# Half 0 alone ahead of the first gate: a reordered start of a block-attention and gated-expert kernel

## The chip, the cores and the metric

The kernel runs on one core of a Trainium2 chip. The metric is the device time of one execution in microseconds (us). Durations of single instructions come from one profiled execution, in which each engine's instructions are recorded: PE (TensorE) multiplies matrices, DVE (VectorE), ACT (ScalarE) and POOL (GpSimd) work elementwise, and SP (SyncE) issues the DMAs.

## The reference

Two parts follow each other. The first is attention with 4 batches, 8 heads, 768 tokens and a head width of 64: a token sees its neighbours at less than 16 places, and 24 summaries, one for each block of 32 tokens (the maximum of the keys, the mean of the values).

```python
k_sum = k.reshape(B, H, nb, block, D).max(axis=3)
v_sum = v.reshape(B, H, nb, block, D).mean(axis=3)
...
scores_all = np.concatenate([scores_l_m, scores_s], axis=-1)
...
a = a / (np.sum(a, axis=-1, keepdims=True) + 1e-09)
return np.matmul(a, v_all).astype(np.float32)
```

The second takes the attention's output as `x`, with 512 features for each token, mixes every token with the one before it, and applies a squared-ReLU pair of products under a sigmoid gate:

```python
xk = mu_k * x + (1.0 - mu_k) * x_prev
xr = mu_r * x + (1.0 - mu_r) * x_prev
k = np.maximum(xk @ w_k, 0.0)
v = k * k @ w_v
r = 1.0 / (1.0 + np.exp(-(xr @ w_r)))
return (r * v).astype(np.float32)
```

`w_k` is 512 x 1024, `w_v` 1024 x 512, `w_r` 512 x 512.

## The kernel before, in words

**Attention.** The heads go in four pairs, two heads of 64 on 128 partitions. For each batch and pair, `load_set` (L310) loads keys into a tile of the pool `kt` (three tiles) and the values of both halves of the tokens into two tiles of `vx`. It adds the block maxima to the keys (L330 to L342) and the block means to the values. For the first batch the means come from PE (L354, with the values of both halves) and a selecting product (L374), through two banks of `mm`, into `vm` and from there by copies (L380) into both value tiles. One `unit` (L394) is a pair and a half of the tokens (384): it loads the queries, makes scores on PE (L415), adds the mask and takes the minimum on DVE (L426), exponentiates on ACT (L430), inverts the sums on DVE (L437), normalises on POOL (L442), transposes on PE (L449), copies on ACT (L453), multiplies by the values on PE (L462) and copies the result out (L473 or L475). A unit needs its pair's keys and both block summaries.

**Gate and experts.** A batch's half (384 tokens, three tiles of 128) is the unit of the second part. `mixes` (L478) makes the mixed input for the gate (`which` 1) or the experts (`which` 0): for each pair a scaling on ACT or POOL (L485, L488), a multiply-add on DVE (L491), a rounded high part on ACT (L494) and the remainder on DVE (L496). The high and low parts stand in `xs`, sixteen buffers, eight for each call; `xa` is the buffer in between. Every product is the sum of three: high by high, high by low, low by high. A gate tile is 12 matmuls into one bank of `mm` (L508 to L510) and a sigmoid into `z` (L514). `experts` (L517) runs eight steps: a first product of 12 matmuls (L529), ReLU, square, split (L534 to L540), and a second of 9 (L550). Three of the four banks of `mm` hold its accumulators, and the fourth serves the first products and any gate tile in between in turn.

**Weights.** The weights arrive as 64-bit words and are turned into a high and a low part by `weight` (L258): a scaling (ACT or POOL), three operations on DVE (L281, L284, L288), a rounding (ACT or POOL) and a subtraction on DVE (L300), for four pieces of `w_r` and eight each of `w_k` and `w_v`. A raw piece waits in one of three `st`.

**Order.** Nothing is ordered by hand. Every operation goes to a planner with a cost (`LENGTH`), and some with a due time; due times are passed backwards to what an operation needs. The planner walks through time, takes on each engine the operation that can start and is due first, and hands out buffers of a pool in the order in which they were asked for. The result is a fixed order for each engine, which the engines follow with semaphores. In the first batch, before the change, the units are due in the order pair 0 half 0, pair 0 half 1, pair 1 half 0 and so on, at `GATES[0] - 2000 - (7 - 2 * p - h) * FIRST`, and all eight are due before the first gate. Half 1's gate tiles stand between the steps of half 0's experts, at the steps in `BETWEEN`.

Of the kernel before, what the change touches and what calls it, by code (L numbers as in the profile page):

```python
# [12 lines left out]
AF = mybir.ActivationFunctionType  # L13
# [4 lines left out]
B, H, S, D = 4, 8, 768, 64  # L18
DM, DF = 512, 1024
BLOCK, WINDOW = 32, 16  # L20
P = 128
NPAIR = H // 2
NS = S // BLOCK
# [3 lines left out]
NK = LK + NS  # L27
KB = QW + NS
KL = NW * KB + 2 * WINDOW
HW = NW // 2  # L30
NSL = HW // 2
HT = S // 2
NTT = HT // P
NCK, NCV = DM // P, DF // P
# [2 lines left out]


LENGTH = dict(
    score=900, transpose=340, vtrans=200, vpool=900, vsel=240, spread=560, spread_p=900, values=1000, gate=2790, gate32=3720, e1=2090, e1_32=2800,  # L40
    e2a=1400, e2b=700, e2=700, e2_32=2800, e2l_32=930,
    kred=860, kred2=470, kmax=190, kcopy=340, vred=860, mask=204, rc=310, evac=475, mixd=535, sub=475, khv=300,
    result=695, wbits=340, wor=612, wsub=612, tiny=60,
# [4 lines left out]
LATENCY = dict(PE=260, DVE=110, ACT=110, POOL=150, SP=0)  # L48
DMA_NS_PER_BYTE = 1 / 340.0
DMA_FIXED = 2000  # L50
GATES = (36000, 46000)
PERIOD = 52000
STEP = 4800
SLACK = 400
COLD = 25000
WR = 0, 6000
EARLY = 15000
FIRST = 4000
UNITS = 6000
BETWEEN = 1, 2, 3  # L60


class Buf:
# [12 lines left out]
class Plan:  # L76
# [4 lines left out]
    def buf(self, pool):  # L81
        n = self.count[pool]
        self.count[pool] = n + 1
        return Buf(pool, n)

    def op(self, eng, cost, due, emit, reads=(), writes=(), size=0, other=None):

        bufs = []
        for x, _ in list(reads) + list(writes):
            if isinstance(x, Buf) and x not in bufs:  # L90
                bufs.append(x)
        ways = {eng: (LENGTH.get(cost, 0), emit)}
        if other:
            ways[other[0]] = (LENGTH[other[1]], other[2])
        o = Op(len(self.ops), ways, due, bufs, size)
        for x in reads:
            o.deps.update(self.writers.get(x, ()))
        for x in writes:
            o.deps.update(self.writers.get(x, ()))
            o.deps.update(self.readers.get(x, ()))  # L100
        for x in reads:
            self.readers.setdefault(x, []).append(o)
        for x in writes:
            self.writers[x] = [o]
            self.readers[x] = []
        o.deps.discard(o)
        for x in bufs:
            x.users.append(o)
        self.ops.append(o)
        o.name = cost  # L110
        return o
# [88 lines left out]
def tile_kernel(ctx: ExitStack, tc: tile.TileContext, q, k, vT, v, mask, ident, pool, sel, mu, w_k, w_v, w_r, out):  # L200
    nc = tc.nc
# [3 lines left out]
    def tiles(name, n, shape, dtype=F32, pool=const):  # L205
        return [pool.tile(shape, dtype, name=f"{name}{i}") for i in range(n)]

    pools = dict(
        kt=tiles("kt", 3, [P, KL]), qt=tiles("qt", 4, [P, HT]), vx=tiles("vx", 12, [P, S + 1]),
        kg=tiles("kg", 2, [P, 49]), ks=tiles("ks", 2, [P, NS]),  # L210
        vs=tiles("vs", 1, [P, NS]), vm=tiles("vm", 4, [P, P]), sp=tiles("sp", 2, [P, P]),
        y=tiles("y", 4, [P, NSL, NK]), mn=tiles("mn", 4, [P, NSL]), sm=tiles("sm", 3, [P, 2 * NSL]),
        rc=tiles("rc", 3, [P, 2 * NSL]), pts=tiles("pts", 3, [NK, NSL, P]),
        z=tiles("z", 6, [P, DM]), xa=tiles("xa", 4, [P, HT]),
        xs=tiles("xs", 16, [P, HT], F32R), r=tiles("r", 2, [P, HT]),
        kh=tiles("kh", 2, [P, HT], F32R), kl=tiles("kl", 2, [P, HT], F32R),
        st=tiles("st", 3, [P, 1024], U32), we=tiles("we", 1, [P, 512], U32), wc=tiles("wc", 2, [P, 512], U32),
# [4 lines left out]
    op, buf = plan.op, plan.buf  # L222
# [10 lines left out]
    wr_h = const.tile([P, NCK, DM], F32R, name="wr_h")  # L233
    wr_l = const.tile([P, NCK, DM], F32R, name="wr_l")
# [10 lines left out]
        out=om_sb, in0=mu_sb, scalar1=-1.0, scalar2=1.0, op0=ALU.mult, op1=ALU.add), reads=MU, writes=OM)  # L245

    def gate_due(b, hf):
        n = 2 * b + hf
        return GATES[n] if n < 2 else GATES[0] + PERIOD * n

    def e1_due(b, hf, j):
        return (GATES[0] + PERIOD * (2 * b + hf)) + 8400 + STEP * j

    def e2_due(b, hf, j):
        return e1_due(b, hf, j + 1) + 2200
# [51 lines left out]
    def windows(vw):  # L307
        return vw.t[0:NK, 0:S].rearrange("p (w d) -> p w d", d=P)

    def load_set(b, p):  # L310

        e = dict(kt=buf("kt"), vw=[buf("vx") for _ in range(2)])
        kt, vw = e["kt"], e["vw"]
        cuts = [0, HW * KB, KL] if (b, p) == (0, 0) else [0, KL]
        for n, (lo, hi) in enumerate(zip(cuts, cuts[1:])):
            op("SP", "load", None, lambda lo=lo, hi=hi: nc.sync.dma_start(out=kt.t[:, lo:hi], in_=k[b, p, :, lo:hi]),
               writes=[(kt, f"k{n}")], size=P * (hi - lo) * 4)
        e["kparts"] = [(kt, f"k{n}") for n in range(len(cuts) - 1)]
        for hf in range(2):
            op("SP", "load", None, lambda hf=hf: nc.sync.dma_start(  # L320
                out=windows(vw[hf]), in_=v[b, p, :, hf * HW:(hf + 1) * HW]),
               writes=[(vw[hf], "a"), (vw[hf], "b")], size=NK * HW * 512)

        def blocks():
# [2 lines left out]
        kg, ks, vm = buf("kg"), buf("ks"), buf("vm")  # L327
        cuts = [0, HW, NW] if len(cuts) > 2 else [0, NW]
        for n, (lo, hi) in enumerate(zip(cuts, cuts[1:])):
            op("DVE", "kred2" if len(cuts) > 2 else "kred", None, lambda lo=lo, hi=hi: nc.vector.tensor_reduce(  # L330
                out=kg.t[:, 4 * lo:4 * hi].rearrange("p (j c) -> p j c", c=4),
                in_=blocks()[:, lo:hi, 0:QW].rearrange("p j (a c) -> p j a c", c=16), op=ALU.max, axis=AX.X),
               reads=[e["kparts"][n]], writes=[(kg, n)])
        op("DVE", "kmax", None, lambda: nc.vector.tensor_reduce(
            out=kg.t[:, 48:49], in_=kt.t[:, NW * KB:NW * KB + 16], op=ALU.max, axis=AX.X),
# [163 lines left out]
            x.append((xh, xl))  # L499
        return x  # L500

    def gate_tile(b, hf, x, z, t):
        ps = buf("mm")
        ts = slice(t * P, (t + 1) * P)

        def products():
            for p, (xh, xl) in enumerate(x):
                nc.tensor.matmul(ps.t, xh.t[:, ts], wr_h[:, p, :], start=(p == 0), stop=False)  # L508
                nc.tensor.matmul(ps.t, xh.t[:, ts], wr_l[:, p, :], start=False, stop=False)  # L509
                nc.tensor.matmul(ps.t, xl.t[:, ts], wr_h[:, p, :], start=False, stop=(p == NPAIR - 1))  # L510

        op("PE", "gate", gate_due(b, hf) + 2800 * t, products, reads=[(a, 0) for pair in x for a in pair]
           + [(("wr", i), s) for i in range(NCK) for s in "hl"], writes=[(ps, 0)])
        op("ACT", "sigmoid", None, lambda: nc.scalar.activation(z[t].t, ps.t, AF.Sigmoid),  # L514
           reads=[(ps, 0)], writes=[(z[t], 0)])

    def experts(b, hf, x, z, between):  # L517

# [80 lines left out]
    for j in range(NCV):  # L599
        weight("wk", j, w_k[:, j * P:(j + 1) * P].rearrange("(c p) n -> p c n", p=P), *places("wk", j))  # L600
        weight("wv", j, w_v[j * P:(j + 1) * P, :], *places("wv", j))
    for p in range(NPAIR):
        e = load_set(0, p)
        for h in range(2):
            unit(0, p, h, e, GATES[0] - 2000 - (7 - 2 * p - h) * FIRST)
    tokens = {}
    for n in range(2 * B):
        b, hf = divmod(n, 2)
        if n not in tokens:
            tokens[n] = mixes(b, hf, 1), [buf("z") for _ in range(NTT)]  # L610
            for t in range(NTT):
                gate_tile(b, hf, *tokens[n], t)
        between = {}
        x = mixes(b, hf, 0)
        if n == 0:

            tokens[1] = mixes(0, 1, 1), [buf("z") for _ in range(NTT)]
            between = {j: [lambda t=t: gate_tile(0, 1, *tokens[1], t)] for t, j in enumerate(BETWEEN)}
        experts(b, hf, x, tokens[n][1], between)
        if hf == 0 and b + 1 < B:  # L620
            for p in range(NPAIR):
                e = load_set(b + 1, p)
                for h in range(2):
                    unit(b + 1, p, h, e, gate_due(b + 1, 0) - 14000 - (7 - 2 * p - h) * UNITS)
# [92 lines left out]
```

## Time and profile before

| | |
|---|---|
| median of three runs | 475.11 us (474.57 to 478.05) |
| the profiled execution | 474.88 us |
| its span, first to last instruction | 473.1 us |
| mean granted TensorE clock | 0.971 |
| PE busy | 445.4 us, 94% of the span |
| DVE busy | 279.3 us, 59% |
| ACT busy | 285.2 us, 60% |
| POOL busy | 121.6 us, 26% |

The page of the profile divides the span into 40 equal slices, with the busy share of each engine in tenths, and lists groups of instructions by line. Views of the trace give busy time in chosen stretches, the instructions in order of time, the waits by who waited for whom, and the chain of work that ended last. In a row of the timeline the first number is the start in us, the second the duration, and what stands in square brackets is idle time of the engine ahead of it and what ended it. Matmuls overlap, so their pace is the distance of starts and not the duration.

### The profile page before, as it was taken

What the parts mean: (1) busy time and instruction counts of PE and PEld (TensorE: products, weight loads), DVE (VectorE), ACT (ScalarE), POOL (GpSimd) and SP (SyncE); (2) the same over time, 40 slices, a digit from 0 to 9 for tenths busy, and PEclk for the clock granted to TensorE, in tenths of its full rate; (3) what the DMA queues carried; (4) which work ended last, traced back from release to release, by engine and by line L of the source; (5) the groups of instructions that cost most, each with busy time, mean ns of one, the idle gap of its engine ahead of it and who ended that gap; (6) DMA issues with size and microseconds to landing.
All of it is one profiled execution on the core that took longest, in us unless ns stands there. A gap on an engine that the chain in (4) does not pass through costs nothing.

```text
span 473.1 us, 9589 instructions
## 1 busy us (share of the span) xinstructions
PE 445.4 (94%) x3476; PEld 372.7 (79%) x3476; DVE 279.3 (59%) x882; ACT 285.2 (60%) x806; POOL 121.6 (26%) x256
## 2 busy tenths in 40 slices
PE   3887898799999999999999999999999999999996
PEld 2565586588888878997778888888778888888995
DVE  4789999969965386339354566338355554222223
ACT  3579784766877566327887657327987655231311
POOL 0659623132434301203242201204142201000000
PEclk9979599979999999999999999999999999999999
DMA  8991437978500219708200217737100010001001
GB/s 250 296 305 60 138 106 220 293 218 250 144 15 15 60 49 276 176 1 266 53 12 10 56 41 220 203 83 242 34 14 8 8 59 10 0 1 67 1 0 67
DMA packets 27013, 51.16 MB, mean 108 GB/s; under 512 B 2903, under 2 KB 14807, under 8 KB 26967
## 3 DMA queue, kind: packets, MB, share of 16 engines
q1 hardware_dynamic: 26967, 50.56, 36.0%
q8 instruction: 27, 0.44, 0.4%
q14 instruction: 19, 0.16, 0.1%
HBM read 42.49 MB, written 6.29 MB: 103 GB/s over the span
## 4 chain that ended last, share of the span: by engine, by line
PE 74%; ACT 8%; DVE 7%; DMA 6%; issue 2%; POOL 2%; SPq 1%; ACTq 0%; DVEq 0%; POOLq 0%
PE mm L550 27%; PE mm L529 26%; PE av L462 4%; PE pt L449 4%; DMA st<-in_w_r 3%; PE mm L508 3%; PE mm L510 3%; PE mm L509 3%; PE sc L415 3%; ACT y L430 2%; DMA kt<-in_k 2%; POOL y L442 2%; ACT L430 1%; DVE we L284 1%; ACT pts L453 1%
## 5 line engine op out<-in xcount | busy, mean ns | idle before, releaser
L442 POOL TENSOR_SCALAR y<-y,rc 128x120 f32<-128x120 f32 x192 | 83.5, 454 | 153.7 <-DVE rc L437 127.7
L529 PE MATMUL mm<-xs,wk_h 128*128 128x384 f32 x512 | 102.4, 342 | 4.1 <-ACT z L514 4.0
L529 PEld LDWEIGHTS mm<-xs,wk_h 128*128 128x128 f32 x512 | 91.5, 190 | 10.2 <-ACT z L514 5.0
L534 ACT ACTIVATE r<-mm 128x384 f32<-128x384 f32 x64 | 31.3, 489 | 94.2 <-PE mm L529 94.1
L430 ACT ACTIVATE y<-y,mn 128x120 f32<-128x120 f32 x192 | 73.7, 386 | 11.9 <-DVE mn L426 11.4
L550 PE MATMUL mm<-wv_h,kh 128*128 128x512 f32 x192 | 78.6, 409 | 0.1
L550 PE MATMUL mm<-wv_l,kh 128*128 128x512 f32 x192 | 75.7, 394 | 0.0
L550 PE MATMUL mm<-wv_h,kl 128*128 128x512 f32 x192 | 59.7, 406 | 0.0
L529 PE MATMUL mm<-xs,wk_l 128*128 128x384 f32 x256 | 55.9, 340 | 0.0
L426 DVE CUSTOM_DVE_ANT_0 y<-sc,mask_sb 128x120 f32<-128x120 f32 x192 | 43.3, 276 | 20.3 <-PE sc L415 17.1
L538 DVE CAST kh<-r 128x384 fp32r<-128x384 f32 x41 | 15.4, 376 | 67.1 <-ACT r L536 67.1
L496 DVE TENSOR_TENSOR xs<-xa,xs 128x384 fp32r<-128x384 f32 x64 | 35.5, 566 | 29.4 <-ACT xs L494 29.3
L529 PEld LDWEIGHTS mm<-xs,wk_l 128*128 128x128 f32 x256 | 46.2, 190 | 0.0
L488 POOL TENSOR_SCALAR xa<-vx,om_sb 128x384 f32<-128x384 f32 x25 | 21.4, 863 | 87.5 <-DVE xs L496 83.3
L491 DVE SCALAR_TENSOR_TENSOR xa<-vx,mu_sb,xa 128x384 f32<-128x384 f32 x64 | 40.8, 658 | 4.3 <-ACT xa L485 2.9
L449 PE MATMUL pt<-ident_sb,y 128*120 128x128 f32 x192 | 37.3, 300 | 5.3 <-ACT pts L453 3.3
L550 PEld LDWEIGHTS mm<-wv_h,kh 128*128 128x128 f32 x192 | 36.1, 188 | 7.7 <-ACT z L514 0.6
L508 PE MATMUL mm<-wr_h,xs 128*128 128x512 f32 x96 | 39.5, 412 | 1.5 <-ACT r L534 1.5
L550 PEld LDWEIGHTS mm<-wv_l,kh 128*128 128x128 f32 x192 | 36.2, 188 | 5.8
L453 ACT COPY pts<-pt 120x384 f32<-120x384 f32 x64 | 30.4, 475 | 16.1 <-PE pt L449 15.7
L550 PEld LDWEIGHTS mm<-wv_h,kl 128*128 128x128 f32 x192 | 34.3, 188 | 6.9 <-DVE kl L540 0.2
L462 PEld LDWEIGHTS av<-pts,vx 120*64 120x64 f32 x768 | 28.9, 147 | 13.6 <-issue 8.4
(60 smaller groups left out, 662.5 us busy)
## 6 DMA issues: line engine op xcount, KB each, us to landing
vx<-in_v SPq DMA_DIRECT2D x32, 360.0 KB
kt<-in_k SPq DMA_DIRECT2D x15, 544.0 KB
qt<-in_q SPq DMA_DIRECT2D x32, 192.0 KB
out<-z SPq DMA_DIRECT2D x24, 256.0 KB
st<-in_vT SPq DMA_DIRECT2D x12, 384.0 KB
st<-in_w_k SPq DMA_DIRECT2D x8, 512.0 KB
st<-in_w_v SPq DMA_DIRECT2D x8, 512.0 KB
st<-in_w_r SPq DMA_DIRECT2D x4, 512.0 KB
```

Source lines behind the costliest of these rows:

```text
L426: op("DVE", "mask", None, lambda h=h, i=i, var=var: nc.vector.tensor_tensor_reduce(out=y[h].t[:, i, :], in0=sc[h].t[:, i, 0:NK], in1=mask_ ...
L430: op("ACT", "exp", None, lambda h=h, i=i: nc.scalar.activation(y[h].t[:, i, :], y[h].t[:, i, :], AF.Exp, bias=mn[h].t[:, i:i + 1], scale=-1.0,
L442: op("POOL", "norm", None, lambda h=h, i=i: nc.gpsimd.tensor_scalar(out=y[h].t[:, i, :], in0=y[h].t[:, i, :], scalar1=rc.t[:, NSL * h + i: ...
L449: nc.tensor.transpose(out=pt[h].t[0:NK, i * P:(i + 1) * P], in_=y[h].t[:, i, :], identity=ident_sb)
L453: op("ACT", "pts", None, lambda h=h: nc.scalar.copy(out=pts[h].t, in_=pt[h].t[0:NK, 0:NSL * P].rearrange("p (i c) -> p i c", c=P)), reads= ...
L462: nc.tensor.matmul(av.t[hs, w * QW:(w + 1) * QW], windows(vw)[:, w, hs], pts[h].t[:, i, c * QW:(c + 1) * QW], start=True, stop=True,)
L491: op("DVE", "mixd", None, lambda xt=xt, xa=xa, p=p: nc.vector.scalar_tensor_tensor(out=xa.t, in0=xt.t[:, 1 + lo:1 + lo + HT], scalar=mu_sb ...
L496: op("DVE", "sub", None, lambda xa=xa, xh=xh, xl=xl: nc.vector.tensor_tensor(out=xl.t, in0=xa.t, in1=xh.t.bitcast(F32), op=ALU.subtract), ...
L508: nc.tensor.matmul(ps.t, xh.t[:, ts], wr_h[:, p, :], start=(p == 0), stop=False)
L529: nc.tensor.matmul(ps.t[:, 0:HT], w[:, j, p, :], x[p][s].t, start=(n == 0), stop=(n == 11))
L534: op("ACT", "relu", None, lambda: nc.scalar.activation(r.t, ps.t[:, 0:HT], AF.Relu), reads=[(ps, 0)], writes=[(r, 0)])
L550: nc.tensor.matmul(acc[t].t, a.t[:, t * P:(t + 1) * P], w[:, j, :], start=start, stop=stop)
```

## The change

Five things are edited. The first batch's units are due half by half: the four of half 0 ahead of the first gate, the four of half 1 after it (5000 apart). The first gate is summed pair by pair: four operations `gate_p`, each with the nine matmuls that one pair gives to the three tiles, with three banks held until all four are done; the sigmoids are due together. All later gates go tile by tile as before; half 1's gate tiles move from steps 1, 2, 3 to steps 5, 6, 7 of half 0's experts, and the due times of half 0's expert steps come earlier. The pool `kt` has four tiles instead of three, `vm` three instead of four, `xa` three instead of four. The values lie in memory half by half, so that one load reads one contiguous piece.

```diff
-GATES = (36000, 46000)
+GATES = (36000, 62000)
...
-FIRST = 4000
+FIRST = 5000
+SECOND = 5000
 UNITS = 6000
-BETWEEN = 1, 2, 3
+BETWEEN = 5, 6, 7
...
-        kt=tiles("kt", 3, [P, KL]), qt=tiles("qt", 4, [P, HT]), vx=tiles("vx", 12, [P, S + 1]),
+        kt=tiles("kt", 4, [P, KL]), qt=tiles("qt", 4, [P, HT]), vx=tiles("vx", 12, [P, S + 1]),
...
-        vs=tiles("vs", 1, [P, NS]), vm=tiles("vm", 4, [P, P]), sp=tiles("sp", 2, [P, P]),
+        vs=tiles("vs", 1, [P, NS]), vm=tiles("vm", 3, [P, P]), sp=tiles("sp", 2, [P, P]),
...
-        z=tiles("z", 6, [P, DM]), xa=tiles("xa", 4, [P, HT]),
+        z=tiles("z", 6, [P, DM]), xa=tiles("xa", 3, [P, HT]),
...
-        return (GATES[0] + PERIOD * (2 * b + hf)) + 8400 + STEP * j
+        return GATES[0] + PERIOD * (2 * b + hf) + (8400 if b or hf else 2000) + STEP * j
...
-                out=windows(vw[hf]), in_=v[b, p, :, hf * HW:(hf + 1) * HW]),
+                out=windows(vw[hf]), in_=v[b, p, hf]),
...
+    def gate(b, hf, x, z, tiles, by_pair=False):
+
+        ps = [buf("mm") for _ in tiles]
+
+        def products(p, i):
+            ts = slice(tiles[i] * P, (tiles[i] + 1) * P)
+            xh, xl = x[p]
+            nc.tensor.matmul(ps[i].t, xh.t[:, ts], wr_h[:, p, :], start=(p == 0), stop=False)
+            nc.tensor.matmul(ps[i].t, xh.t[:, ts], wr_l[:, p, :], start=False, stop=False)
+            nc.tensor.matmul(ps[i].t, xl.t[:, ts], wr_h[:, p, :], start=False, stop=(p == NPAIR - 1))
+
+        def needs(p):
+            return [(a, 0) for a in x[p]] + [(("wr", p), s) for s in "hl"]
+
+        if by_pair:
+            for p in range(NPAIR):
+                op("PE", "gate_p", gate_due(b, hf) - (NPAIR - p) * 3000,
+                   lambda p=p: [products(p, i) for i in range(len(tiles))], reads=needs(p), writes=[(a, 0) for a in ps])
+        for i, t in enumerate(tiles):
+            if not by_pair:
+                op("PE", "gate", gate_due(b, hf) + 2800 * t, lambda i=i: [products(p, i) for p in range(NPAIR)],
+                   reads=[a for p in range(NPAIR) for a in needs(p)], writes=[(ps[i], 0)])
+            op("ACT", "sigmoid", None if not by_pair else gate_due(b, hf) + 8000,
+               lambda i=i, t=t: nc.scalar.activation(z[t].t, ps[i].t, AF.Sigmoid),
+               reads=[(ps[i], 0)], writes=[(z[t], 0)])
...
-    for p in range(NPAIR):
-        e = load_set(0, p)
-        for h in range(2):
-            unit(0, p, h, e, GATES[0] - 2000 - (7 - 2 * p - h) * FIRST)
+    sets = [load_set(0, p) for p in range(NPAIR)]
+    for hf in range(2):
+        for p in range(NPAIR):
+            unit(0, p, hf, sets[p], GATES[0] - 5000 - (3 - p) * FIRST if hf == 0 else GATES[0] + 5000 + SECOND * p)
...
-            for t in range(NTT):
-                gate_tile(b, hf, *tokens[n], t)
+            gate(b, hf, *tokens[n], range(NTT), by_pair=(n == 0))
...
+    vn = vn.reshape(B, NPAIR, NK, 2, HW, P).transpose(0, 1, 3, 2, 4, 5)
```

More of the change, by code (lines that the diff above doesn't have):

```diff
@@ L39 @@
 LENGTH = dict(
-    score=900, transpose=340, vtrans=200, vpool=900, vsel=240, spread=560, spread_p=900, values=1000, gate=2790, gate32=3720, e1=2090, e1_32=2800,
+    score=900, transpose=340, vtrans=200, vpool=900, vsel=240, spread=560, spread_p=900, values=1000, gate=2790, gate_p=2100, gate32=3720, e1=2090, e1_32=2800,
     e2a=1400, e2b=700, e2=700, e2_32=2800, e2l_32=930,
@@ L500, in mixes @@
         return x
[L502 to L515, printed above, removed]
+    def gate(b, hf, x, z, tiles, by_pair=False):
[19 more added lines that the diff above has]
+               reads=[(ps[i], 0)], writes=[(z[t], 0)])
     def experts(b, hf, x, z, between):
@@ L617, in tile_kernel @@
             tokens[1] = mixes(0, 1, 1), [buf("z") for _ in range(NTT)]
-            between = {j: [lambda t=t: gate_tile(0, 1, *tokens[1], t)] for t, j in enumerate(BETWEEN)}
+            between = {j: [lambda t=t: gate(0, 1, *tokens[1], [t])] for t, j in enumerate(BETWEEN)}
         experts(b, hf, x, tokens[n][1], between)
```

## The prediction, before the result was known

> **What bounds it now.** I read the page's head and slices first, then busy time by stretches, the timeline of TensorE, and the chain that ended last.
>
> ```profile
> span 473.1 us, 9589 instructions
> PE   3887898799999999999999999999999999999996
> 0.00:36.00 36.00, 23.60 (x344) 16.73 (x344) 24.93 (x111) 20.87 (x81) 16.34 (x39) 0.91 0.96 283
> 36.00:56.00 20.00, 15.49 (x191) 10.54 (x192) 18.98 (x62) 16.28 (x58) 18.65 (x30) 0.76 0.22 64
> 56.00:96.00 40.00, 34.30 (x167) 27.16 (x165) 38.13 (x79) 29.54 (x58) 8.23 (x10) 0.93 0.68 219
> 96.00:116.00 20.00, 20.00 (x113) 17.94 (x112) 17.05 (x43) 12.57 (x33) 5.62 (x11) 0.88 0.79 236
> 0.00:116.00 116.00, 93.39 (x808) 72.37 (x809) 99.09 (x291) 79.26 (x228) 48.84 (x89) 0.88 0.71 215
> ```
>
> The columns of a stretch are its length, then PE, weight loads, DVE, ACT, POOL busy, the granted clock, DMA share and GB/s. After 100 us PE is full and nothing done there can be hidden; whatever is won must be won before. Three limits follow each other. Until 36 us it is the DMA (share 0.96). From 36 to 56 it is POOL and DVE together (18.65 and 18.98 of 20). From 56 to 96 it is DVE (38.13 of 40), which splits the weights for the experts.
>
> ```profile
> 56.33 0.80 PE L508 MATMUL mm<-wr_h,xs 128*128 128x512 f32 x1
> 60.39 0.40 PE L509 MATMUL mm<-wr_l,xs 128*128 128x512 f32 x1
> 63.19 0.40 PE L509 MATMUL mm<-wr_l,xs 128*128 128x512 f32 x1
> 66.46 1.58 PE L529 MATMUL mm<-xs,wk_h 128*128 128x384 f32 x8
> ...
> 103.23 2.09 PE mm L550 x9
> 105.31 2.12 PE mm L529 x12
> 181.53 4.16 PE mm L529 x24
> 287.53 4.24 PE mm L529 x24
> ```
>
> The first four are from the timeline, the rest from the chain. The first gate starts at 56.33, the first expert product at 66.46. Twelve gate matmuls at full clock take 2.80 (60.39 to 63.19), so a gate of three tiles costs 8.4. One expert step costs 2.1 + 2.1, eight of them 33.5. A whole batch takes 287.53 - 181.53 = 106.0; less two gates and two expert passes (83.8) leaves 22.2 for eight attention units, 2.8 each.
>
> From this I make a PE ledger. At 181.53 the second batch's experts begin. Going back over the experts of half 1 (33.5), eight units (22.2) and one gate (8.4), that is 64.1, half 0 with both its gates is accounted for at **117.4**. Going forward from 66.46, PE needed 8.4 + 33.5 = 41.9, which is 108.4. So 9.0 us were lost in between, and this is what the largest piece looks like:
>
> ```profile
> 93.39 1.28 ACT L514 ACT_TABLE_LOAD   x1
> 94.69 0.60 ACT L514 ACTIVATE z<-mm 128x512 f32<-128x512 f32 x1
> 95.33 2.93 PE L529 MATMUL mm<-xs,wk_h 128*128 128x384 f32 x8 [3.99 <-ACT z L514]
> 99.47 1.48 PE L415 MATMUL sc<-kt,qt 64*64 64x120 f32 x24
> 100.88 1.65 PE L529 MATMUL mm<-xs,wk_h 128*128 128x384 f32 x8
> ...
> PE mm L529 <- ACT z L514: 4.0, 1, 4.0
> ```
>
> The last line is from the view of the waits: this happened once. Three of the four banks `mm` hold the accumulators, so a gate tile and the next first product share one. The sigmoid that frees it stood behind exponentials and a table load. PE idled 3.99, then ran at half clock until 100.88: 5.55 us for a first product and a score group that take 2.1 + 0.8 at full clock, so 2.6 more. One such event costs 6.6.
>
> **The change, part by part.** *First gate earlier.* Four units leave the path. What they held is read on POOL and in the means of the operations.
>
> ```profile
> 21.45 10.85 DMA kt<-in_k
> 40.59 3.44 POOL L442 TENSOR_SCALAR y<-y,rc 128x120 f32<-128x120 f32 x6 [0.89 <-DVE rc L437]
> 45.16 4.04 POOL L442 TENSOR_SCALAR y<-y,rc 128x120 f32<-128x120 f32 x6
> 50.08 3.50 POOL L442 TENSOR_SCALAR y<-y,rc 128x120 f32<-128x120 f32 x6
> L453 ACT COPY pts<-pt 120x384 f32<-120x384 f32 x16 | 7.6, 475 | 4.3 <-PE pt L449 4.2
> L475 ACT COPY vx<-av 128x384 f32<-128x384 f32 x6 | 2.8, 472 | 1.3 <-PE av L462 1.3
> L485 ACT ACTIVATE xa<-vx,om_sb 128x384 f32<-128x384 f32 x10 | 6.1, 616 | 0.8 <-DVE om_sb L244 0.8
> L494 ACT CAST xs<-xa 128x384 fp32r<-128x384 f32 x13 | 6.6, 506 | 0.0
> L491 DVE SCALAR_TENSOR_TENSOR xa<-vx,mu_sb,xa 128x384 f32<-128x384 f32 x16 | 11.3, 715 | 1.0 <-ACT xa L485 1.0
> L496 DVE TENSOR_TENSOR xs<-xa,xs 128x384 fp32r<-128x384 f32 x12 | 7.2, 603 | 0.1
> ```
>
> The normalisations run in the order of the units: 40.59 is pair 2's half 1, 45.16 pair 3's half 0, 50.08 pair 3's half 1. Half 0 of pair 3 thus ends at 49.2 behind one unit that goes, and the earlier half-1 units stood ahead of it too. Pair 3's keys landed at 32.30 (21.45 + 10.85). The loads ahead of the gate hardly shrink, because the block means (L354) read both value halves: only four query loads move behind.
>
> ```profile
> vx<-in_v SPq DMA_DIRECT2D x32, 360.0 KB
> kt<-in_k SPq DMA_DIRECT2D x15, 544.0 KB
> qt<-in_q SPq DMA_DIRECT2D x32, 192.0 KB
> st<-in_w_r SPq DMA_DIRECT2D x4, 512.0 KB
> ```
>
> Four key sets, eight value halves, four gate weights and four queries are 7.9 MB (in 1024s), 28.5 us at the 283 GB/s of the first stretch, so about 31 us with the start. Pair 3's half 0 is then the fourth normalisation and not the seventh: I put its end at 40, between 37 (31 + scores and softmax of some 6) and 49.2 (as now). Behind it come transposes and two copies (2 x 0.475, with PE 2.5), values 1.5, the copy out 0.47, the mix 0.62 + 0.72 + 0.51 + 0.60, and hand-overs, together some 8. Of the gate only the last pair's nine matmuls remain (2.1), because the other three pairs' parts ran ahead. So the first expert product comes at **S = 50**, 16.5 earlier than now, and between 46 and 58. The gate's three banks are taken in turn after those of pair 3's block means, so its first part cannot start before pair 3's values are in; that leaves nine microseconds for three parts of 2.1. On SP the four queries of half 1 (192 KB, 0.7 us each at 283 GB/s) now stand among the expert weights; with a DMA share of 0.22 from 36 to 56 there is room, at worst 2.8 us of delay to the first weight.
>
> *Half 1 moves behind S.* PE gets 4 x 2.8 = 11.2 more to do there. The ledger reads 50 + 41.9 + 11.2 = 103.1 plus losses. Queued behind each `gate_p` on PE are later pairs' transposes and values; if a mix is late they wait with it, which is why I keep S up to 58.
>
> *Losses, and DVE as their source.* The last weight is split at 115.96 now:
>
> ```profile
> 115.28 0.68 DVE L300 TENSOR_TENSOR wv_l<-wc,wv_h 128x512 fp32r<-128x512 f32 x1
> L426 DVE CUSTOM_DVE_ANT_0 y<-sc,mask_sb 128x120 f32<-128x120 f32 x12 | 3.3, 273 | 1.7 <-PE sc L415 1.7
> L330 DVE TENSOR_REDUCE kg<-kt 128x48 f32<-128x768 f32 x2 | 1.9, 940 | 0.0
> L366 DVE TENSOR_REDUCE vs<-st 128x24 f32<-128x768 f32 x1 | 0.9, 934 | 0.0
> ```
>
> These groups of 56 to 116 belong to the next batch; with their small helpers and the four mixes of half 1's experts (4 x 0.6) they make about 9 of DVE's 99.1 busy us. So 90 us must be done before the last weight, in either version, and DVE's idle time was 11.1 by 36 us and 5.8 after. If DVE stayed as idle early and lost 3 later, the last weight would be ready at 90 + 11 + 3 = 104. The weights become due 6.4 us earlier in the planner's terms (8400 to 2000), the next batch's units do not, so more of the 9 falls behind; I take half, 108.5, and 2.1 for the last second product: 110.6. Both ways meet when PE's losses are 8, at **111.1**: one stall by a sigmoid (6.6) and 1.5 for the mix of half 1. That mix now waits for the last gate tile at step 7 to give back its `xs`, with 2.1 + 4.2 of PE work to cover some 7.
>
> *Keys kept, fewer `vm` and `xa`.* A fourth `kt` takes away a wait for a buffer; since the DMA is full until 36, I give it nothing beyond S. Three `xa` for four cost between 0 and two mixes (1.2); three `vm`, freed by the copies L380, the same; I take 0, covered by DVE being the slower engine of that pipe. *Values by halves.* Rows stay 3072 B long at their destination; no row compares the layouts. The 2.9 MB of the first batch take 10.4 us at 283 GB/s, and the page's first three slices moved 250, 296 and 305 GB/s, so I bound it by a tenth, 1 us either way, and take 0.
>
> ```profile
> GB/s 250 296 305 60 138 106 220 293 218 250 144 15 15 60 49 276 176 1 266 53 12 10 56 41 220 203 83 242 34 14 8 8 59 10 0 1 67 1 0 67
> ```
>
> *Table loads.* The change puts half 0's sigmoids between exponentials of both halves, one pair of loads more there, 2 x 1.28, and perhaps two pairs at the gate tiles at steps 5 to 7. ACT was idle 10.5 of 40 us from 56 to 96, which covers 2.6, and covers 7.7 only where no bank waits. The Trainium skill, "ScalarE: Activation LUTs", Rules for kernel authors, says to do all functions of one table set before switching, and counts 2.66 us a switch with the drain; here the sigmoid began 1.30 after its load, so the trace carries 1.28 alone. By the page's figure the three pairs would be an estimated 16 us of ACT, more than that idle time.
>
> **Sum.** 117.4 - 111.1 = 6.3 us, all ahead of the full stretch, which moves up whole. The profiled execution took 474.88, its span 473.1 and 1.78 around it; the median of the three runs is 475.11. 474.88 - 6.3 = **468.5**.
>
> **Rivals.** *DVE gives nothing back* (0.22): the next batch's DVE work still slips between the weights and the last weight comes at 113 to 116 as now. Then 115 to 118 against 117.4, a time of 472.5 to 475.5. For it: DVE was busy 38.13 of 40 where the experts now run. Against it: 11 us of DVE's idle lay before 36. *Three sigmoid stalls* (0.14): at steps 5, 6 and 7 each gate tile's bank waits behind exponentials that wait for DVE masks. Two events beyond the one counted cost 13.2, less 6.3, so 481.8, slower; it decides from the second event. For it: row 93.39, where this happened at the only tile that had exponentials just ahead of it; the skill's rule above is this mechanism, and by its 2.66 us each event would be an estimated 1.4 us dearer. Against it: the other two tiles (steps 1 and 2) did not stall (the waits show one case), and the next batch's exponentials may not be there yet. *DVE at its floor* (0.12): last weight at 104, so 106.1 and 463.6.
>
> **Numbers.** My forecast, 464.5 to 471.5, has 0.52. Under 1% (4.75 us) this kernel cannot be told from no change: its three runs spread over 3.5. Faster by over 1% is 0.45 of the forecast plus the floor, 0.57; slower is 0.14 and 0.02 of the first rival, 0.16; the rest 0.27. The range 460 to 479 reaches from the floor (with the layout's and S's bounds) to just under the three stalls.
>
> **What would show it.** Right: gate rows in groups of nine from 34 to 48, the first expert product near 50, the last `wv_l` subtraction near 108, at most one PE idle of 3 or more before a first product, and the second batch's experts at 175. Wrong: first product after 58 (mixes late on DVE), the last subtraction still at 114 or later, several PE waits for `z` between 80 and 110, or a wait for `xs` ahead of half 1's experts.

## The result, and the profile after

The changed kernel takes **477.25 us** (median of 20 runs, 476.32 to 481.25), the kernel before 475.37 (20 runs, 473.13 to 478.05). The ratio is 1.0051, 95% interval 1.0035 to 1.0067: half a per cent, or 1.9 us by the medians, slower. Forecast was 468.5, a gain of 6.3. The profiled execution took 476.72.

The page's head and the busy time by stretches of the changed kernel (columns as before: length, PE, weight loads, DVE, ACT, POOL, clock, DMA share, GB/s):

```profile
span 474.9 us, 9572 instructions
PE   1779877879999999999999999999999999999996
0.00:36.00 36.00, 19.40 (x286) 13.24 (x286) 25.89 (x94) 19.38 (x69) 13.66 (x32) 1.00 0.98 293
36.00:56.00 20.00, 18.40 (x174) 13.56 (x174) 18.92 (x53) 14.02 (x47) 16.91 (x25) 0.91 0.30 89
56.00:96.00 40.00, 31.69 (x229) 24.73 (x227) 36.09 (x89) 31.81 (x75) 21.32 (x29) 1.00 0.60 194
96.00:116.00 20.00, 17.54 (x101) 14.28 (x102) 17.87 (x43) 15.88 (x33) 5.90 (x10) 1.00 0.75 228
0.00:116.00 116.00, 87.03 (x787) 65.82 (x788) 98.77 (x276) 81.09 (x219) 57.79 (x94) 0.99 0.69 213
```

The full stretch now begins after 116 us and not at 100: from 96 to 116 PE is busy 17.54 of 20 where it was busy all 20 before. DVE's sum to 116 us is as before (98.77 and 99.09). The timeline of TensorE, and last its first row of the second batch's experts from the chain:

```profile
37.47 0.80 PE L510 MATMUL mm<-wr_h,xs 128*128 128x512 f32 x1
42.26 0.48 PE L510 MATMUL mm<-wr_h,xs 128*128 128x512 f32 x1
47.20 0.50 PE L510 MATMUL mm<-wr_h,xs 128*128 128x512 f32 x1
53.73 0.50 PE L510 MATMUL mm<-wr_h,xs 128*128 128x512 f32 x1
57.56 2.19 PE L541 MATMUL mm<-xs,wk_h 128*128 128x384 f32 x8
...
96.17 1.68 PE L541 MATMUL mm<-xs,wk_h 128*128 128x384 f32 x8 [1.25 <-ACT z L526]
106.19 1.63 PE L541 MATMUL mm<-xs,wk_h 128*128 128x384 f32 x8 [1.76 <-ACT z L526]
...
183.13 4.16 PE mm L541 x24
```

The change did what it says. The gate ran in four groups, begun at 37.47, 42.26, 47.20 and 53.73, and the first expert product came at 57.56, 8.9 us earlier than before (66.46). The second batch's experts nevertheless begin at 183.13, 1.6 later. So 10.5 us went between these two points. How many of half 1's units were done by then is read from the exponentials of ACT, six to a unit and 48 in the batch, here up to 36 us and from 36 to 57.5:

```profile
L431 ACT ACTIVATE y<-y,mn 128x120 f32<-128x120 f32 x24 | 9.2, 385 | 3.9 <-DVE mn L427 3.9
L431 ACT ACTIVATE y<-y,mn 128x120 f32<-128x120 f32 x13 | 5.0, 388 | 2.4 <-DVE mn L427 2.4
```

The exponential that ran across 36.0 stands in both rows, so 36 of 48 were done and 12 were left, two units at 2.8 us of PE, 5.6. In the ledger of the prediction: 183.13 - 64.1 = 119.0 is 57.56 + 41.9 + 5.6 and **14.0 us of losses**. Before it was 66.46 + 41.9 + 9.0 = 117.4. The first product gave 8.9, the units took 5.6, the losses 5.0 more. (PE's own rows put a little more behind 57.56: the scores of one unit, the transposes of two and a half, the values of three. That is an estimated 6.3, which would make the losses 13.3.)

Where PE lost them, from 57.5 to 120 us (total, times, longest), and what ACT did ahead of the sigmoid at step 6 (rows of its timeline):

```profile
PE mm L541 <- ACT z L526: 3.0, 2, 1.8
PE mm L562 <- DVE kh L550: 2.4, 1, 2.4
PE pt L450 <- POOL y L443: 2.3, 4, 1.1
PE mm L510 <- ACT r L546: 1.7, 2, 1.2
```

```profile
101.65 0.68 ACT L275 ACTIVATE wc<-st 128x512 f32<-128x512 f32 x1 [1.46 <-DVE wk_l L301]
102.35 1.28 ACT L431 ACT_TABLE_LOAD   x1
103.64 0.40 ACT L431 ACTIVATE y<-y,mn 128x120 f32<-128x120 f32 x1
104.15 1.28 ACT L526 ACT_TABLE_LOAD   x1
105.44 0.60 ACT L526 ACTIVATE z<-mm 128x512 f32<-128x512 f32 x1
106.06 1.28 ACT L431 ACT_TABLE_LOAD   x1
```

Five ACT instructions from 101.65 to 106.04 do 1.68 us of arithmetic and 2.56 of table loads, and PE waits at their end for the shared bank. Counted in ACT's timeline up to 116 us, the changed kernel has loaded tables eight times, the kernel before five times. Only one wait is of DVE's making directly, but the last weight's split still starts at 111.47, 3.8 us earlier than before (115.28), against the 9 us by which the experts began earlier:

```profile
111.47 0.69 DVE L301 TENSOR_TENSOR wv_l<-wc,wv_h 128x512 fp32r<-128x512 f32 x1
```

### The profile page after: what moved, and what is told of

Read it like the earlier page. It is cut to its first block, busy times and chain, and to the rows that moved or that the text cites. A ratio compares the mean times of both kernels' runs of the same rounds, so it can differ in the third digit from the quotient of the medians.

```text
span 474.9 us, 9572 instructions
## 1 busy us (share of the span) xinstructions
PE 439.7 (93%) x3476; PEld 366.5 (77%) x3476; DVE 277.9 (59%) x875; ACT 292.8 (62%) x815; POOL 128.8 (27%) x258
## 4 chain that ended last, share of the span: by engine, by line
PE 69%; ACT 9%; DVE 6%; POOL 6%; DMA 5%; issue 2%; SPq 1%; POOLq 0%; ACTq 0%; DVEq 0%
PE mm L562 25%; PE mm L541 24%; POOL y L443 5%; PE av L463 4%; PE mm L510 3%; PE pt L450 3%; DMA vx<-in_v 3%; PE mm L512 3%; PE mm L511 3%; PE sc L416 3%; ACT y L431 3%; ACT L431 2%; DMA st<-in_w_k 2%; DVE xa L492 1%; ACT pts L454 1%
## 5 line engine op out<-in xcount | busy, mean ns | idle before, releaser
L443 POOL TENSOR_SCALAR y<-y,rc 128x120 f32<-128x120 f32 x192 | 90.0, 487 | 133.6 <-DVE rc L438 118.9
L541 PEld LDWEIGHTS mm<-xs,wk_h 128*128 128x128 f32 x512 | 90.2, 188 | 10.1 <-issue 2.8
L416 PE MATMUL sc<-kt,qt 64*64 64x120 f32 x768 | 30.2, 285 | 13.6 <-DVE kt L343 7.6
L450 PE MATMUL pt<-ident_sb,y 128*120 128x128 f32 x192 | 35.3, 288 | 7.3 <-ACT pts L454 3.7
L489 POOL TENSOR_SCALAR xa<-vx,om_sb 128x384 f32<-128x384 f32 x18 | 14.7, 824 | 92.9 <-DVE xs L497 92.9
L552 DVE TENSOR_TENSOR kl<-r,kh 128x384 fp32r<-128x384 f32 x64 | 36.4, 568 | 4.7 <-ACT kh L551 1.9
```

The costliest lines, as they stand in the source:

```text
L416: nc.tensor.matmul(sc[h].t[cs, i, 0:NK], qt.t[hs, n * QW:(n + 1) * QW], kt.t[hs, w * KB:w * KB + NK], start=True, stop=True,)
L443: op("POOL", "norm", None, lambda h=h, i=i: nc.gpsimd.tensor_scalar(out=y[h].t[:, i, :], in0=y[h].t[:, i, :], scalar1=rc.t[:, NSL * h + i: ...
L450: nc.tensor.transpose(out=pt[h].t[0:NK, i * P:(i + 1) * P], in_=y[h].t[:, i, :], identity=ident_sb)
L541: nc.tensor.matmul(ps.t[:, 0:HT], w[:, j, p, :], x[p][s].t, start=(n == 0), stop=(n == 11))
L552: op("DVE", "sub", None, lambda: nc.vector.tensor_tensor(out=kl.t, in0=r.t, in1=kh.t.bitcast(F32), op=ALU.subtract), reads=[(r, 0), (kh, 0 ...
```

## The experiments

Each ratio is to the kernel before on the same chip (medians 475.1 to 476.0); medians of different rows can be of different chips, so kernels are compared by their ratios where the two disagree. The kernels with copies, without the sign operations or with a third of a gate leave that work out and are there for their time alone; all others compute everything.

| kernel | median us | ratio, 95% interval |
|---|---|---|
| changed kernel | 477.25 | 1.0051 (1.0035 to 1.0067) |
| changed, sigmoids of batch 0 as copies | 472.26 | 0.9942 (0.9904 to 0.9980) |
| before, the same | 471.87 | 0.9941 (0.9909 to 0.9973) |
| changed, 20 sign operations left out | 472.47 | 0.9954 (0.9922 to 0.9985) |
| before, the same | 469.18 | 0.9875 (0.9827 to 0.9924) |
| changed, copies and no sign operations | 469.64 | 0.9845 (0.9787 to 0.9903) |
| before, the same | 466.33 | 0.9802 (0.9756 to 0.9848) |
| before, layout of the values alone | 475.16 | 0.9978 (0.9949 to 1.0006) |
| changed, a third of half 1's gate matmuls | 479.76 | 1.0077 (1.0046 to 1.0108) |
| before, the same | 475.68 | 1.0002 (0.9970 to 1.0034) |
| changed, first gate tile by tile | 476.19 | 1.0014 (0.9987 to 1.0042) |
| changed, old order of units | 474.25 | 0.9967 (0.9940 to 0.9994) |
| changed, old order, gate tile by tile | 475.95 | 1.0005 (0.9976 to 1.0033) |
| before, gate tiles at steps 5 to 7 | 479.29 | 1.0085 (1.0053 to 1.0117) |
| before, the same with due time 62 | 477.59 | 1.0029 (1.0003 to 1.0055) |
| before, expert steps due 6.4 earlier | 475.18 | 1.0001 (0.9974 to 1.0027) |
| before, gate as tanh | 469.88 | 0.9876 (0.9819 to 0.9934) |
| changed, gate as tanh | 470.21 | 0.9883 (0.9830 to 0.9937) |
| changed, old order, gate as tanh | 468.73 | 0.9854 (0.9817 to 0.9891) |

**Table loads and DVE work, each taken away from both kernels.** First the sigmoids of the first batch became copies, which need no table of their own:

```diff
-  nc.scalar.activation(z[t].t, ps[i].t, AF.Sigmoid),
+  nc.scalar.activation(z[t].t, ps[i].t, AF.Sigmoid if b else AF.Copy),
```

> The changed kernel, with the sigmoids of batch 0 (both halves) made plain copies, so those z are left out as gates; the order of every engine is the same, only eight table loads go. Theory A (table loads and the one shared bank hold PE up after the first expert product): the waits of PE for z and for kh (3.0 and 2.4 us) mostly go, second batch's experts at 179 instead of 183.1, time 473 (4 us under the changed kernel's 477.25). Theory B (DVE's supply of split weights holds it up): PE waits elsewhere instead, at most 1 us is won, 476.5.

> The kernel before, with the same replacement (batch 0's sigmoids as copies; four table loads go). Theory A: the one stall of 4.0 us and the half clock behind it go, 4 to 6 us won, 470 to 471. Theory B: under 1 us, 474.5.

The loads are worth 5.0 us in the changed kernel (477.25 - 472.26) and 3.3 in the kernel before (475.13 on that chip, less 471.87). The second is less than the 4 to 6 expected and half of the 6.6 at which the prediction had priced the one stall; the wait there shrinks from 4.0 to 1.9 and doesn't go. Without the loads the two kernels are level by their middle values (0.9942 and 0.9941), but each interval is over 0.7% wide, and the loss to be explained is 0.51%. In the changed kernel the trace shows where the time comes back, as theory A had it: PE's waits for a sigmoid and for `kh` fall from 3.0 and 2.4 to these, and the second batch's experts begin 4.5 earlier (183.13):

```profile
PE mm L541 <- ACT z L526: 0.4, 1, 0.4
PE mm L562 <- DVE kh L550: 0.4, 1, 0.4
...
178.63 4.16 PE mm L541 x24
```

Then DVE was relieved of one of its four operations on each weight:

```diff
-  nc.vector.scalar_tensor_tensor(out=we.t, in0=words()[0], scalar=0x80000000, in1=we.t, ...)
+  return
```

> The changed kernel without the operation that puts the sign into each weight piece (20 DVE instructions of some 0.6 us left out, so 12 us of DVE work less before the last weight; the weights' signs are left out of the result). Theory B: last weight some 8 to 10 us earlier and 6 us or more won, 471 or less. Theory A: DVE was not what PE waited for, under 2 us won, 475.5 to 477.

> The kernel before without the same 20 DVE instructions. Theory B: 5 us or more won, 470 or less. Theory A: the path to the first gate holds two or three of them (1 to 2 us), the rest is slack, 473 to 474.

Both gain, the kernel before more (6.0 against 4.8). In the changed kernel, which lands between the two theories, the last weight's split starts 4.4 us earlier (107.08) and not 8 to 10, and PE still waits 2.4 for `kh` and 2.0 for sigmoids: not DVE alone holds it. Then both together:

> The changed kernel with both: batch 0's sigmoids as copies, and the weights' sign operation left out. If table loads and DVE's supply are two separate holds, their gains add: 477.2 - 5.0 - 4.8 = 467.5. If each only uncovers the other or something third, less: 470 to 472. Theory C (below) says that a third one is left, the late gate tiles, so that this stays above 467.

> The kernel before with batch 0's sigmoids written as copies (no table load for them) and the 20 sign operations of DVE left out: the same two cuts that the changed kernel had for 469.6. In before each cut alone gave 3.3 and 6.0. Theory A (the stages before the second batch are paced by how fast weights are split on DVE and handed on through ScalarE, so each cut counts on its own): 475.5 - 3.3 - 6.0 = about 466, three to four below the changed kernel with the same cuts, so the new order loses by itself. Theory B (one floor below, the same for both orders, is reached once either cost is gone): 468 to 470, level with the changed kernel; then the new order costs nothing and the whole loss lies in the extra table loads and the DVE queue.

In the kernel before the gains add up (466.33, 8.9 below, where the single ones make 9.3). In the changed one they fall short by the medians (7.6 against 9.8) and add up by the ratios (2.06% and 2.06%), so whether they overlap there stays open. The medians lie 3.3 apart with the kernel before ahead, the ratios 0.43%; the intervals overlap. The profiled executions agree on the sign, the second batch's experts starting at 175.96 in the changed and at 172.85 in the kernel before:

```profile
175.96 4.16 PE mm L541 x24
172.85 4.16 PE mm L529 x24
```

So under no condition that was tried is the changed kernel ahead of the kernel before. DVE's share of the time is seen in the changed kernel with copies, from 57.5 to 123.5 us:

```profile
57.50:123.50 66.00, 59.61 (x463) 47.97 (x464) 63.41 (x178) 47.74 (x134) 30.99 (x50) 1.00 0.69 217
```

DVE, the third busy time after PE and the weight loads, is busy 63.41 of 66 once ACT's loads are gone: that is probably the next limit, and it is one that an earlier first product doesn't move.

**The layout alone.**

```diff
-  in_=v[b, p, :, hf * HW:(hf + 1) * HW]),
+  in_=v[b, p, hf]),
```

> The kernel before with only the values laid out by halves; every engine's order is the same. I took 0 within 1 us either way: 474 to 476. Were the layout worth something in the DMA-bound first 36 us, 473 or less.

Nothing beyond the measurement's uncertainty.

**Is it PE's time at the later steps?** Of each of half 1's three gate tiles, eight of the twelve matmuls were left out, 5.6 us of PE in all.

```diff
+  if (b, hf) != (0, 1):
       nc.tensor.matmul(... xh, wr_h ...)
       nc.tensor.matmul(... xh, wr_l ...)
   nc.tensor.matmul(... xl, wr_h ...)
```

> The changed kernel with 4 of the 12 matmuls in each of half 1's three gate tiles (batch 0), so 24 matmuls or 5.6 us of PE work at steps 5 to 7 left out. Theory C: by being moved to steps 5 to 7 these tiles stand behind PE's idle time, no longer in it, so nearly all comes back: 472 to 472.5. Theories A and B: PE is held up by something else at these steps, 2 us or less come back, 475 or more.

> The kernel before with the same 24 matmuls left out, there at steps 1 to 3. Theory C: they filled time in which PE waited for DVE anyway, under 2 us are won, 473.5 or more. If PE's work counts wherever it stands, 5.6 us: 469.5.

Less work on PE wins nothing in either; the changed kernel's median is even 2.5 higher (the intervals overlap). Two rows of its TensorE timeline and one of its waits say why (its lines stand one lower):

```profile
96.77 2.83 PE L542 MATMUL mm<-xs,wk_h 128*128 128x384 f32 x8 [2.35 <-ACT z L527]
108.08 2.90 PE L542 MATMUL mm<-xs,wk_h 128*128 128x384 f32 x8 [3.39 <-ACT z L527]
PE mm L542 <- ACT z L527: 6.8, 3, 3.4
```

The sigmoids come no earlier, PE waits 6.8 instead of 3.0, and what follows these two waits runs at half clock: the granted clock is 0.54 from 96.7 to 99.6 us and 0.50 from 108 to 111, and the rows take 2.83 and 2.90 where the changed kernel, at 1.00 there, has 1.68 and 1.63. The way through DVE, ACT and the bank sets the pace there, not PE.

**The first gate tile by tile.**

```diff
-  gate(b, hf, *tokens[n], range(NTT), by_pair=(n == 0))
+  gate(b, hf, *tokens[n], range(NTT), by_pair=False)
```

> The changed kernel with its first gate summed tile by tile as all the other gates are, not pair by pair; only half 0's units ahead of it, the kept keys and the layout stay. Theory A (the pair-by-pair sum brings the three sigmoids together, with one table load pair, but starts the first expert product no earlier, since the last pair is what it waits for): within 1 us of the changed kernel, 476 to 478. Theory B (the partial sums done ahead are worth their PE time behind the last pair, about 5.6 us of gate products less 1.5): 480 to 482.

The time is theory A's, the reason isn't: in the new order the pair-by-pair sum brings the first product from 64.20 to 57.56 and wins nothing (1.0051 with it, 1.0014 without). That was the first sign that this product's time is not what counts.

**Which part does what.** Five kernels take the parts apart. First the old order of the units in the changed kernel:

```diff
-  for hf in range(2):
-      for p in range(NPAIR):
-          unit(0, p, hf, sets[p], GATES[0] - 5000 - (3 - p) * FIRST if hf == 0 else GATES[0] + 5000 + SECOND * p)
+  for p in range(NPAIR):
+      for hf in range(2):
+          unit(0, p, hf, sets[p], GATES[0] - 2000 - (7 - 2 * p - hf) * 4000)
```

> The changed kernel with the units of the first batch back in the order before (both halves of a pair, one after the other, all ahead of the first gate); the gate is still summed pair by pair, the keys kept, half 1's gate tiles at steps 5 to 7. Theory A (putting half 1's units behind the first gate takes PE work out of the first 36 us, where PE is idle anyway, and so gives back what the earlier first product wins): PE's busy time up to 36 us returns from 19.4 to some 22 to 23.5, the first expert product comes at 62 to 66, and the time is 473 to 476, below the changed kernel by 1 to 4. Theory B (the order is what wins, the rest of the change loses): 479 to 483.

The time is theory A's; whether its reason is can't be told. By 36 us PE was busy 23.51 us here against 19.40, as the theory has it, but only 26 exponentials have begun against 24, and the tanh form of the same order (below), the fastest kernel of all, was busy 19.15 by then. By 57.5 us this kernel has all of half 1's exponentials done. So none of them stands behind the first sigmoids, and six table loads are made by 116 us instead of eight. With the gate summed pair by pair, the half-by-half order with its due times costs 0.84%, 4.0 us, and the two intervals don't touch. Next half 1's gate tiles alone:

```diff
-  BETWEEN = 1, 2, 3
+  BETWEEN = 5, 6, 7
```

> The kernel before with one part of the change alone: half 1's gate tiles stand at expert steps 5 to 7 instead of 1 to 3. Theory A (there they meet the next batch's exponentials and ScalarE's in-order queue, which was the changed kernel's loss): two or three waits for a sigmoid of 2 us and more, 478 to 481. Theory B (the steps do not matter, the loss in the changed kernel comes from its emptier first 36 us): 474.5 to 476.5, with table loads as before.

The time is theory A's, 4.0 us by the ratio. At steps 1 to 3 the tiles lay in time that PE had to spare (in the kernel before, leaving out two thirds of them won nothing); at 5 to 7 they meet the next batch's exponentials. But from 57.5 to 120 us the waits for sigmoids come to 3.2 us in all, less than the 4.0 of the one stall before. New are waits of the second products, for `kh` above all, the longest of them at 89.05 and thus ahead of the moved tiles' sigmoids:

```profile
89.05 0.50 PE L550 MATMUL mm<-wv_h,kh 128*128 128x512 f32 x1 [3.34 <-DVE kh L538]
99.12 1.66 PE L529 MATMUL mm<-xs,wk_h 128*128 128x384 f32 x8 [1.23 <-ACT z L514]
109.98 1.75 PE L529 MATMUL mm<-xs,wk_h 128*128 128x384 f32 x8 [1.93 <-ACT z L514]
...
PE mm L550 <- DVE kh L538: 3.3, 1, 3.3
PE mm L529 <- ACT z L514: 3.2, 2, 1.9
PE mm L550 <- DVE kl L540: 1.6, 1, 1.6
PE mm L550 <- ACT kh L539: 1.2, 2, 1.0
```

So the loss is shown, and theory A's reason for it in part at most.

Two more kernels asked what makes that good again in the old order: the expert steps' due time alone, and the old order without the pair-by-pair sum.

```diff
-  return (GATES[0] + PERIOD * (2 * b + hf)) + 8400 + STEP * j
+  return GATES[0] + PERIOD * (2 * b + hf) + (8400 if b or hf else 2000) + STEP * j
```

> The kernel before with one number of the change alone: the first expert steps fall due 6.4 us earlier in the planner, so the weights' splits on DVE come ahead of more of the next batch's work. Theory A (the earlier due time is what won the 5 us between half 1's gate tiles moved alone and the whole change in the old order): 470 to 472. Theory B (the pair-by-pair gate won them): 474.5 to 476.

> The changed kernel in the old order of the units and with the first gate tile by tile. Against the same with the gate pair by pair (474.3) theory A, the due times won it: 474 to 475.5, no difference. Theory B, the pair-by-pair sum wins in the old order although the first product starts no earlier, since PE's gate work is done while it waits for units: 477.5 to 480.

The due time alone does nothing. Without the pair-by-pair sum the old order comes to 1.0005 where it had 0.9967; the intervals overlap, so its 1.8 us are likely and not shown. This kernel also limits what was said of the order: with the gate tile by tile the new order stands at 1.0014 and the old at 1.0005, no difference that can be told. The 0.84% is the cost of the order together with the pair-by-pair sum, which seems to help in the old order and to harm in the new. And the kernel settles another point. Its first expert product and the split of its last weight, from the timeline, and its second batch, from the chain:

```profile
71.80 1.38 PE L541 MATMUL mm<-xs,wk_h 128*128 128x384 f32 x7
111.26 0.69 DVE L301 TENSOR_TENSOR wv_l<-wc,wv_h 128x512 fp32r<-128x512 f32 x1
183.10 4.24 PE mm L541 x24
```

The first product is 14.2 us later than in the changed kernel (57.56), and the second batch begins at the same time (183.10 and 183.13). No unit of half 1 is left behind it, so in the ledger 119.0 is here 71.80 + 41.9 and 5.3 of losses, against 14.0. The last weight's split starts at the same time too (111.26 and 111.47). Last, the gate tiles moved together with their due time:

```diff
-  GATES = (36000, 46000)
+  GATES = (36000, 62000)
...
-  BETWEEN = 1, 2, 3
+  BETWEEN = 5, 6, 7
```

> The kernel before with half 1's gate tiles at steps 5 to 7 and their due time at 62 us instead of 46, as in the change. With the tiles moved alone the due time stayed at 46, so their mixes on DVE kept their place ahead of the weights although the tiles came later. Theory A (that was the loss of 3.3): 474.5 to 477, level with the old order by tile (475.9). Theory B (the place of the tiles itself loses, and the kept keys or the earlier expert steps make it good in the old order): 478.5 to 481.

1.0029, between the two theories: some of the loss was probably the old due time (the intervals just meet), 1.4 us of it remain. The wait of 3.3 for `kh` is gone in this trace; the sigmoids' waits are still 3.1. What the kept keys add to it wasn't tried alone.

**Without table loads and with everything computed.** As sigmoid(x) = (tanh(x/2) + 1)/2, the gate can be had from tanh. The half goes into the square, the one into the last multiplication.

```diff
-  nc.scalar.activation(z[t].t, ps.t, AF.Sigmoid)
+  nc.scalar.activation(z[t].t, ps.t, AF.Tanh, scale=0.5)
...
-  nc.scalar.activation(r.t, r.t, AF.Square)
+  nc.scalar.activation(r.t, r.t, AF.Square, scale=0.5**0.5)
...
-  nc.vector.tensor_tensor(out=z[t].t, in0=acc[t].t, in1=z[t].t, op=ALU.mult)
+  nc.vector.scalar_tensor_tensor(out=z[t].t, in0=z[t].t, scalar=1.0, in1=acc[t].t, op0=ALU.add, op1=ALU.mult)
```

> The kernel before with sigmoid(x) computed as (tanh(x/2)+1)/2, all units: ScalarE takes tanh where it took sigmoid, the square carries the factor one half, and the last DVE operation of each tile adds one and multiplies. If tanh lies in the table set of the exponentials, the four loads of the first 116 us that the sigmoids cause go without leaving anything out: theory A (table loads price the gate) 471 to 472.5, as with the copies (471.9). Theory B (tanh has a set of its own here, or the copies won time in another way): 474.5 to 476.

> The changed kernel with the same tanh form, everything computed. Theory A (the eight table loads of the first 116 us instead of five are what turns the change into a loss): 471.5 to 473, level with the kernel before in the tanh form within 1 us. Theory B (the loss lies in the order of the units): it stays 1.5 to 2 above the kernel before in the tanh form.

> The changed kernel with the old order of the units and the gate as tanh, everything computed. Theory A: as the old order keeps the first 36 us filled and the tanh form has no table loads left, 466 to 469, the fastest of all. Theory B (one floor for all orders once the loads are gone): 469.5 to 471, level with the other two kernels in the tanh form.

All three beat both kernels, the first two by more than theory A had; the last, at 468.73 or 0.9854, is the fastest, but the three intervals overlap. The changed kernel gains 7.0 and is level with the kernel before in the same form. The one table load of its trace, and its chain:

```profile
0.73 1.28 ACT L275 ACT_TABLE_LOAD   x1 [0.73 <-PEq L719]
179.04 4.24 PE mm L541 x24
284.09 4.24 PE mm L541 x24
389.13 4.24 PE mm L541 x24
```

With sigmoids the changed kernel loaded 22 times in all. 4.1 us are won before the second batch (183.13 to 179.04), with PE's waits for a sigmoid and for `kh` down to 0.4 and 0.5 as with the copies. The two later batches take 105.05 and 105.04 where the changed kernel with sigmoids took 106.01 and 106.09; that the sigmoids cost about a microsecond in each later batch too had been counted nowhere. The Trainium skill, "ScalarE: Activation LUTs", Table sets: the hidden batching unit, lists tanh in the table set of exp as well as in that of sigmoid; the single load above agrees.

## Why the prediction was wrong, point by point

- **The sum of S and the units came within 2.0 us, by luck: two errors nearly cancel.** S was forecast at 50 (46 to 58) and came at 57.56; the units behind it were to be 11.2 and were 5.6. Together 63.2 against 61.2.
- **Why S was late.** Pair 3's half 0 was normalised by 42.5 instead of 40, which is close:

```profile
32.88 3.77 POOL L443 TENSOR_SCALAR y<-y,rc 128x120 f32<-128x120 f32 x6 [0.42 <-DVE mn L427]
39.52 2.97 POOL L443 TENSOR_SCALAR y<-y,rc 128x120 f32<-128x120 f32 x6
```

  From there to S the forecast had 10 us (8, and 2.1 for the gate's last part) and the trace has 15. I summed the durations of a free pipe, but DVE was busy 18.92 of the 20 us from 36 to 56, and PE and ACT worked on half 1's first two units in between. That is also why fewer units were left behind.
- **The step that failed is "Losses": taken at 8, measured at 14.0.** It was forecast as one stall of 6.6 and 1.5. No single event was as dear: the two sigmoid waits together make 3.0. The rest is a sum of small waits, for `kh`, for a normalisation, for a ReLU, each at the end of a hand-over in the queue of ACT, DVE or POOL.
- **Behind it stands a wrong model.** The ledger let S, the units and the losses be chosen apart. They are not: S at 57.56 with 14.0 of losses and S at 71.80 with 5.3 end at the same time, the last weight's split starting at 111.47 and 111.26. The reading that fits both: an expert step needs its weights, and DVE's order and ACT's hand-overs bring them when they bring them; what S gains comes back as waiting. Why ACT and DVE bring them no earlier in the changed kernel was not taken apart further.
- **DVE's ledger.** Last weight at 108.5 (floor 104) was forecast, 112.2 came (111.47 + 0.69); 2.1 us from there to the last second product were forecast, and the product's last matmul started at 121.39, 9.2 later. The first part is half of what I gave. The second was never 2.1: the kernel before itself took 6.4 (115.96 to 122.34), which its trace would have shown. The rest of it is in part the bank's hand-overs (step 7's first product starts at 114.11, behind the third gate tile and its sigmoid), which I had placed in the other ledger alone. That the two ledgers came to 110.6 and 111.1 was taken as support, and was none.
- **Table loads.** Three more came by 116 us, where I had one pair and perhaps two more; the price was wrong: I let ACT's idle time cover them. An idle share says nothing about an instruction on which PE waits. That the loads cost the changed kernel about 1% in the first batch is shown by the copies, and tanh agrees. Taking them away also levels the middle values of the two kernels, both times, so the loss against before is likely theirs in the main; but the intervals are as wide as that loss, and with DVE relieved as well the two part again (0.9845 and 0.9802). Their number alone is no price, since the old order by tile has eight loads as well and is level with before: what counts is what waits behind them.
- **Rivals.** The three stalls had the right mechanism and steps (5 to 7) and the right sign; at 481.8 the size was too great by 4.6, since two of them cost 3.0 in waiting and none fell to half clock. DVE giving nothing back held in part: last weight 3.8 earlier, no more. A slower kernel had been given 0.16.
- **Right.** Layout 0 (0.9978, interval across 1); the gate's groups from 37.47 on; no wait for `xs` ahead of half 1's experts. The kept keys, `vm` and `xa` at nothing were not tried alone.

By parts, as ratios to before: half 1's gate tiles moved alone +0.85%, with their due time +0.29%; the rest of the change in the old order and by tile brings it to +0.05%, the pair-by-pair sum to -0.33%, and the half-by-half order, the part that the gain was to come from, to +0.51%. Only the first and the last of these steps are clear of their intervals, and the sizes hang on the order of the steps: with the order changed first, by tile, it goes to +0.14%, and the pair-by-pair sum then adds the rest. In the tanh form the two orders, by pair, differ by 0.29% (0.9883 and 0.9854, intervals overlapping). That would fit an order whose 4.0 us went in part by way of table loads; how much of it, and whether anything remains, stays open.

## What to carry to other kernels

Before a start is moved earlier, ask what supplies the work behind it; if a supply on another engine has its own pace, the start is not a term of the sum, and two ledgers that agree are no proof as long as both leave out the same hand-overs. Price a function that switches ACT's table by what waits behind it and not by ACT's idle share, and look first for a form of it in the set already loaded: here that was worth 5 to 7 us, more than any order of the units that was tried.

## What the runs showed of the hardware

Less work made PE slower in two places. With 5.6 us of gate matmuls gone, PE idled 2.35 and 3.39 us ahead of two first products, and these took 2.83 and 2.90 at granted clocks of 0.54 and 0.50. With the matmuls in place it idled 1.25 and 1.76 us there, and they took 1.68 and 1.63 at a clock of 1.00. So idle time had taken PE to half clock, and work which filled these waits was not only free but kept the clock. The Trainium skill, "TensorE: Matmul & The Clock Gate", What's actually happening, puts the idle window at about 3.4 us; the wait of 2.35 is shorter than that, so here a shorter one was enough, or it fell together with others ahead of it, which no run tells apart.
